# A gated causal convolution on one core: sixteen small GpSimd operations move to VectorE, and all queues get a new order

## The chip, the cores and the metric

The kernel runs on one core of a Trainium2 chip. The core has a matrix engine (TensorE, "PE" in the profile, with its weight loads as "PEld"), three elementwise engines (VectorE, "DVE"; ScalarE, "ACT"; GpSimd, "POOL") and a queue that only issues transfers (SyncE, "SP"). Each works through its own list of instructions in order, and they wait for one another through semaphores. The metric is the device time of one execution in microseconds (us); less is better.

## The reference

```python
def reference(x, w, w_o):              # x [2, 16000, 144], w [15, 144, 288], w_o [144, 144], bf16
    B, T, D = x.shape
    K = w.shape[0]; dil = 2; pad = (K - 1) * dil
    xp = jnp.pad(x, ((0, 0), (pad, 0), (0, 0)))
    h = jnp.einsum('btc,cd->btd', xp[:, pad:pad + T, :], w[0])
    for i in range(1, K):
        off = pad - i * dil
        h = h + jnp.einsum('btc,cd->btd', xp[:, off:off + T, :], w[i])
    f = h[..., :D]; g = h[..., D:]
    z = jnp.tanh(f) * _sigmoid(g)
    return z @ w_o
```

A causal convolution along time with 15 taps that lie two steps apart, from 144 channels to 288; tanh of one half times the sigmoid of the other; then a 144 by 144 projection.

## The kernel before

**Tiling.** The 32000 time steps are cut into 128 runs of 250, one for each partition, so a "tile" is one time step of all 128 runs. Of the 144 channels the first 128 fill the contraction of a matmul (tiles named XA); the 16 that are left over, called the odd ones here, are packed from eight time steps into one contraction of 128 (tiles named XB). Work goes by octets of eight steps; two octets make a pair, and each pair has two "units", one for the even and one for the odd steps in it.

**Fewer multiplications.** The convolution is computed with nested differences: sums of weights (WC, WS, WT, WD, WV) are formed once in the opening, differences of tiles (V, DU, DD, and across octets GX, GU, GV, GD) are formed by VectorE for each octet (L736, L806, L813, L818), and products that several outputs share are computed once on TensorE (all at L824) and spread: ScalarE copies a PSUM bank to another (L977), or evicts it to SBUF (L450 for two neighbouring banks in one instruction, L453 for two that do not lie side by side), and VectorE adds shared parts (L1004, L1078). GpSimd does the large adds UX (L1014, two to a unit, 60 in all).

**Gate and projection.** ScalarE evicts each finished pair of banks with sigmoid and tanh (TG), VectorE multiplies (Z, L851), a DMA transposes Z to ZT (L917), TensorE projects (L934), ScalarE evicts to OS (L877) and a DMA stores it (L945).

**How x comes in.** After an opening that loads x and the weights in five pieces each and transposes on TensorE (L592 to L606), x comes in chunks of 16 steps (Xr, L489). For each octet the 128 full channels are copied to a staging tile (STA) and transposed by DMA into XA (L691). For each chunk the 16 odd channels are packed into a tile C16: two of six columns are plain copies (`free_copy`, recorded at L877 as C<-Xr), and four are differences of steps two apart, which GpSimd computes at L668 (C<-Xr 128x256, 15 times). C16 is transposed by DMA (L670), written to a scratch tensor in DRAM (L678) and read back in the layout of XB (L703). In the opening a copy of 128x512 from XBh to XB stands on GpSimd (L634), in front of the first XB transfers.

**What sets the order.** The whole program is first written down as a graph of 2617 operations with their reads and writes. The order on each of the five queues is a list of operation numbers, worked out beforehand and kept in the source (`TABLE`, L20 to L94). `ON_ACT` (L95) names those `free_copy` operations that go to ScalarE instead of VectorE. When the program is built, `place` runs through the lists with assumed durations (`dur`, and for transfers `DMA_LAT`, `DMA_RATE` and `FIRST`); from this it takes which physical PSUM bank each product gets. Waits follow from the data alone: each operation waits for whatever wrote what it reads, and each queue is strictly in order, so an operation that waits holds up everything behind it on its engine. The flag `lock` marks operations which the planning keeps from overlapping between VectorE and GpSimd.

Of the kernel before, what the change touches and what calls it, by code (L numbers as in the profile page):

```python
# [5 lines left out]
ACT = mybir.ActivationFunctionType  # L6
ALU = mybir.AluOpType
# [5 lines left out]
DMA_LAT = 3.2  # L13
DMA_RATE = 280e3
FIRST = (1.12, 1.5)
# [78 lines left out]
}  # L94
ON_ACT = (110, 218, 275, 428, 430, 588, 908, 1067, 1227, 1393, 1702, 1704, 2023, 2182)  # L95


class _Op:
# [251 lines left out]
def _conv_wavenet_kernel(nc, x, w, w_o, out):  # L350
# [38 lines left out]
    with contextlib.ExitStack() as st:  # L389
# [74 lines left out]
        def bslot(o):  # L464
            return (o + 1) % NB
# [406 lines left out]
        def free_copy(dst, src, r, w, dur, alt):  # L872
            op = g.add("dve", lambda e: cast(op.eng, dst, src)(e), r=r, w=w, dur=dur, lock=True)
            op.alt = alt
# [514 lines left out]
```

## Time and profile before

| | |
|---|---|
| median of 3 runs | 308.64 us (308.09 to 308.67) |
| the profiled execution | 309.4 us |
| its span, first to last instruction | 307.6 us |
| granted TensorE clock | 1.00 of full speed |
| busy: TensorE, VectorE, ScalarE, GpSimd | 300.8, 279.9, 266.4, 111.4 us |
| matmuls | 2556 |

The profile records one execution. A row of the timeline reads: start, duration, engine, line of the kernel, operation, what is written from what, shape, count; in square brackets the time that the engine was idle before it and what ended the wait. `SPq` is the transfer queue at work. A busy time of TensorE overlaps from one matmul to the next, so its gaps are better seen in the starts.

### The profile page before, as it was taken

The numbers are of one execution on the slowest core, as the hardware profiler recorded it, in microseconds if no ns is written. First come the engines' busy times: TensorE is split into PE (matmuls) and PEld (weight loads), VectorE is DVE, ScalarE is ACT, GpSimd is POOL, SyncE is SP. The second block draws the span as 40 slices with busy tenths as digits, with TensorE's granted clock in tenths as the row PEclk, the third lists the DMA queues.
The fourth block names the chain that finished last, engine by engine and source line by source line (L and its number), as shares of the span: only waits on it lengthen the run. The fifth ranks groups of instructions, "written<-read, shape, count | busy, mean of one in ns | idle before, by whom it ended". The sixth has DMA issues, their size and how long they took to land.

```text
span 307.6 us, 7370 instructions
## 1 busy us (share of the span) xinstructions
PE 300.8 (98%) x2556; PEld 233.9 (76%) x2556; DVE 279.9 (91%) x604; ACT 266.4 (87%) x774; POOL 111.4 (36%) x105
## 2 busy tenths in 40 slices
PE   8899999999999999999999999999999999999995
PEld 7676677777677878877787788777777777877784
DVE  2999999999999999999998999999989799999755
ACT  2588799998879999998998999898898989988885
POOL 3494341333541244333224334313334332133330
PEclk9999999999999999999999999999999999999999
DMA  7959789989749999897767497977829997540543
GB/s 203 311 112 211 145 205 176 226 229 175 210 106 232 184 248 220 180 242 161 215 134 197 135 204 200 187 179 195 165 64 261 172 152 189 140 117 12 143 105 127
DMA packets 96719, 54.38 MB, mean 177 GB/s; under 512 B 83421, under 2 KB 86797, under 8 KB 96683
## 3 DMA queue, kind: packets, MB, share of 16 engines
q1 hardware_dynamic: 96137, 53.54, 77.2%
q0 software_dynamic: 512, 0.33, 0.5%
q8 instruction: 20, 0.33, 0.4%
q14 instruction: 16, 0.13, 0.1%
q10 hardware_dynamic: 34, 0.05, 0.1%
HBM read 15.93 MB, written 10.69 MB: 87 GB/s over the span
## 4 chain that ended last, share of the span: by engine, by line
PE 83%; DVE 10%; DMA 3%; SPq 1%; issue 1%; ACT 0%; DVEq 0%
PE PS L824 74%; PE PS L934 9%; DMA WA<-in_w_dram 2%; DMA XA<-STA 2%; DVE DD L736 1%; DVE V L736 1%; DVE DU L736 1%; DVE WC L646 1%; SPq L489 1%; DVE Xp L1004 1%; DVE Z L851 1%; DVE PS L1078 1%; DVE GU L806 1%; DVE WT L646 1%; DVE WD L646 0%
## 5 line engine op out<-in xcount | busy, mean ns | idle before, releaser
L1014 POOL TENSOR_TENSOR UX<-UC,XS 128x576 f32<-128x576 f32 x60 | 83.7, 1416 | 170.9 <-ACT UC L450 103.6
L824 PE MATMUL PS<-WB,XB 128*128 128x288 bf16 x360 | 102.2, 286 | 0.0
L824 PE MATMUL PS<-WA,GD 128*128 128x288 bf16 x450 | 88.3, 287 | 0.2
L977 ACT ACTIVATE PS<-PS 128x288 f32<-128x288 f32 x213 | 82.1, 415 | 4.4 <-PE PS L824 2.9
L450 ACT ACTIVATE TG<-PS 128x288 bf16<-128x288 f32 x204 | 73.0, 415 | 6.4 <-PE PS L824 5.3
L877 ACT ACTIVATE OS<-PS 128x432 bf16<-128x432 f32 (+1 forms) x93 | 42.7, 492 | 15.5 <-PE PS L934 14.9
L1004 DVE TENSOR_TENSOR Xp<-PS,UD 128x576 f32<-128x576 f32 x60 | 43.1, 751 | 10.7 <-PE PS L824 9.3
L1078 DVE TENSOR_TENSOR PS<-PS,Xp 128x288 f32<-128x288 f32 x120 | 50.8, 459 | 2.2 <-PE PS L824 0.6
L824 PEld LDWEIGHTS PS<-WA,GD 128*128 128x128 bf16 x450 | 41.0, 98 | 14.4 <-DVE PS L1078 1.6
L1078 DVE TENSOR_TENSOR PS<-PS,UX 128x288 f32<-128x288 f32 x120 | 50.0, 457 | 0.6
L824 PE MATMUL PS<-WS,GU 128*128 128x288 bf16 x210 | 44.6, 286 | 0.4 <-DVE GU L806 0.4
L934 PE MATMUL PS<-WOR,ZT 128*128 128x144 bf16 (+1 forms) x322 | 42.0, 254 | 0.0
L824 PEld LDWEIGHTS PS<-WB,XB 128*128 128x128 bf16 x360 | 35.2, 98 | 8.8
L824 PE MATMUL PS<-WC,GV 128*128 128x288 bf16 x210 | 37.8, 286 | 0.0
L824 PE MATMUL PS<-WD,DD 128*128 128x288 bf16 x210 | 34.7, 287 | 0.0
L934 PEld LDWEIGHTS PS<-WOR,ZT 128*128 128x128 bf16 x322 | 27.7, 98 | 6.2 <-issue 0.3
L851 DVE TENSOR_TENSOR Z<-TG 128x576 bf16<-128x576 bf16 (+1 forms) x63 | 28.1, 451 | 2.8 <-ACT TG L450 2.3
L736 DVE TENSOR_TENSOR V<-XA 128x1024 bf16<-128x1024 bf16 (+2 forms) x38 | 24.8, 655 | 0.1
L824 PE MATMUL PS<-WT,DU 128*128 128x288 bf16 x120 | 24.4, 287 | 0.4 <-DVE WT L646 0.4
L824 PEld LDWEIGHTS PS<-WD,DD 128*128 128x128 bf16 x210 | 19.6, 98 | 6.5 <-ACT PS L977 1.0
L824 PEld LDWEIGHTS PS<-WS,GU 128*128 128x128 bf16 x210 | 20.1, 98 | 5.9 <-DVE GU L806 0.7
L824 PE MATMUL PS<-WC,GX 128*128 128x288 bf16 x120 | 23.6, 286 | 0.0
(101 smaller groups left out, 437.5 us busy)
## 6 DMA issues: line engine op xcount, KB each, us to landing
Xr<-in_x_dram SPq DMA_DIRECT2D x15, 648.0 KB, 4.9
out_dram<-OS SPq DMA_DIRECT2D x30, 288.0 KB, 2.9
XB<-XB SPq DMA_DIRECT2D x29, 288.0 KB, 3.4
XB<-s SPq DMA_DIRECT2D x60, 48.0 KB, 3.0
s<-T SPq DMA_DIRECT2D x15, 96.0 KB, 3.0
WA<-in_w_dram SPq DMA_DIRECT2D x2, 288.0 KB, 5.5
ZT<-Z SPq DMA_TRANSPOSE x32, 3.4
Xp<-in_x_dram SPq DMA_DIRECT2D x2, 252.0 KB, 4.8
```

Source lines behind the costliest of these rows:

```text
L450: return e.activation(bass.AP(t[:].tensor, off + (0 if st > 0 else n), [[row, NP], [st, 2], [1, n]]), bass.AP(PS[:].tensor, lo * 512 + c0, ...
L489: return e.dma_start(tile_ap, src)
L646: g.add(eng, lambda v: v.tensor_tensor(dst(), a(), b(), ALU.add), r=r, w=wk, dur=dur, lock=True)
L736: return g.add("dve", lambda v: v.tensor_tensor(dst(), a(), b(), ALU.subtract), r=r, w=wk, dur=dur, prio=2, lock=True)
L824: return lambda t: t.matmul(bank(b), lhsT=lhs(), rhs=rhs(), start=start, stop=True, skip_group_check=True)
L851: g.add("dve", lambda v: v.tensor_tensor(dst(), TG[:, s, 1, 2 * k:2 * k + n, :], TG[:, s, 0, 2 * k:2 * k + n, :], ALU.mult), r=[("TG", s, ...
L877: return (lambda e: e.activation(dst(), src(), ACT.Copy)) if eng == "act" else (lambda e: e.tensor_copy(dst(), src()))
L934: return t.matmul(PS[:, c0:c0 + n * D], lhsT=ZT[:, zt, blk_, :], rhs=WOR[:, wi_:wi_ + n, :].rearrange("p a b -> p (a b)"), start=first, st ...
L977: g.add("act", lambda e: e.activation(bank(c), bank(b), ACT.Copy), r=[("bank", b)], w=[("bank", c)], dur=0.29, prio=prio)
L1004: return v.tensor_tensor(ue(u % NU, q, 0, 2).rearrange("p (v n) -> p v n", v=2), src, UD[:, u % NUD, :, :], ALU.add)
L1014: op = g.add("pool", lambda p: p.tensor_tensor(UX[:, u % NU, h, :, :], UC[:, 0, :, :], bass.AP(XS[:].tensor, h * N2, [[2 * N2, NP], [0, 2] ...
L1078: g.add("dve", lambda e, dst=dst, src=src, ua=ua: e.tensor_tensor(bank(dst), bank(src), ua(), ALU.add), r=[("bank", src), ("UX", us, h) if ...
```

## The change

Three things.

1. The subtraction of the odd channels (15 times) is recorded for VectorE, not GpSimd.
2. The 128x512 copy of the opening becomes a `free_copy`, an operation that stands on VectorE unless `ON_ACT` names its number. Its number is 82, and the new `ON_ACT` holds 82. `ON_ACT` as a whole goes from 14 to 18 numbers: of the octet copies to STA it names ten (four before), of the small copies to C16 seven (ten before).
3. All five lists are new, with the planning constants changed. GpSimd's list keeps the memsets, the 16 small weight transfers in another order, and the 60 large adds; its opening part has neither subtractions nor the copy. The functions `free_copy` and `cast` only move up in the source.

```diff
-DMA_LAT = 3.2
+DMA_LAT = 2.9
+SMALL = 1.45
 DMA_RATE = 280e3
-FIRST = (1.12, 1.5)
+FIRST = (1.12, 1.3)
...
-    "act": ("3 4 36 5 33 43 51 35 63 53 61 72 71 81 143 79 107 108 110 122 113 121 171 95 94 173 175 218 100 99 18 104 ...
+    "act": ("3 4 36 5 33 35 51 53 63 43 61 18 72 71 79 81 108 107 110 122 113 121 82 218 171 100 99 143 173 175 94 95 104 ...
...
-    "dve": ("1 0 30 31 34 146 41 42 155 138 130 131 156 144 132 52 157 133 139 149 134 140 163 135 136 62 150 147 148 141 137 158 160 ...
+    "dve": ("1 0 30 31 34 41 42 155 130 139 132 131 52 157 144 138 146 149 160 133 156 147 163 150 140 62 136 141 134 158 159 166 ...
...
-ON_ACT = (110, 218, 275, 428, 430, 588, 908, 1067, 1227, 1393, 1702, 1704, 2023, 2182)
+ON_ACT = (82, 110, 218, 430, 437, 590, 908, 915, 1065, 1225, 1227, 1234, 1393, 1543, 1545, 1702, 1711, 2021)
...
-            g.add("pool", lambda p: p.tensor_copy(XB[:, bslot(0), :, 0:2, :], XBh[:, 4:12, :].rearrange("p (a b) c -> p a b c", a=2)[:, :, 0:2, :]),
-                  r=[("XBh", 0)], w=[("XB", bslot(0), 0)], dur=0.7, lock=True)
+            free_copy(lambda: XB[:, bslot(0), :, 0:2, :], lambda: XBh[:, 4:12, :].rearrange("p (a b) c -> p a b c", a=2)[:, :, 0:2, :], [("XBh", 0)], [("XB", bslot(0), 0)], 0.2, 0.53)
...
-            g.add("pool", lambda p: p.tensor_tensor(cc[:, :, :, 2:6], xr(2), xr(0), ALU.subtract), r=[("Xr", s)], w=[("C16", s, 1)], dur=0.7, lock=True)
+            g.add("dve", lambda v: v.tensor_tensor(cc[:, :, :, 2:6], xr(2), xr(0), ALU.subtract), r=[("Xr", s)], w=[("C16", s, 1)], dur=0.56, lock=True)
...
-                  r=[("STA", q, 0), ("STA", q, 1)], w=[("XA", s)], dur=1.3, dma="xa", nbytes=8 * 128 * 128 * 2)
+                  r=[("STA", q, 0), ("STA", q, 1)], w=[("XA", s)], dur=1.3, dma="xa", nbytes=SMALL * 8 * 128 * 128 * 2)
```

`SMALL` multiplies the assumed size of the transfers that move 256-byte pieces (the three kinds of transposes and the write of S16); it stands only in the planning. In the lists above, 18 is the small activation that fetches the sigmoid table (L534), 33, 51, 61 and 71 are evictions of transposed XA tiles, 52 and 62 the memsets behind two of them (L606), 130 to 153 sums of weights (L646), and 155 to 169 the first tile differences (L736 to L818). In the parts left out, the subtractions stand in VectorE's list at places 36, 44 and 62 (the first three) and then 2 to 58 places apart; on SP the transposes, loads and stores change places with their neighbours, most by fewer than six.

More of the change, by code (lines that the diff above doesn't have):

```diff
@@ L608, in transposes, with free_copy, cast @@
             compact_pro(pi)
+        def free_copy(dst, src, r, w, dur, alt):
+            op = g.add("dve", lambda e: cast(op.eng, dst, src)(e), r=r, w=w, dur=dur, lock=True)
+            op.alt = alt
+        def cast(eng, dst, src):
+            return (lambda e: e.activation(dst(), src(), ACT.Copy)) if eng == "act" else (lambda e: e.tensor_copy(dst(), src()))
         hk = ["XBc_h%d" % i for i in range(5)]
@@ L667, in compact_chunk @@
             free_copy(lambda: cc[:, :, :, 0:2], lambda: xr(2, 2), [("Xr", s)], [("C16", s, 0)], 0.2, 0.31)
-            g.add("pool", lambda p: p.tensor_tensor(cc[:, :, :, 2:6], xr(2), xr(0), ALU.subtract), r=[("Xr", s)], w=[("C16", s, 1)], dur=0.7, lock=True)
+            g.add("dve", lambda v: v.tensor_tensor(cc[:, :, :, 2:6], xr(2), xr(0), ALU.subtract), r=[("Xr", s)], w=[("C16", s, 1)], dur=0.56, lock=True)
             if ci:
-                g.add("sp", lambda e: e.dma_start_transpose(T16[:, s, :, :], C16[:, s, :, :, :].rearrange("p a b c -> p (a b c)")), r=[("C16", s, 0), ("C16", s, 1)], w=[("T16", s)], dur=1.3, dma="xb", nbytes=3 * 32768)
+                g.add("sp", lambda e: e.dma_start_transpose(T16[:, s, :, :], C16[:, s, :, :, :].rearrange("p a b c -> p (a b c)")), r=[("C16", s, 0), ("C16", s, 1)], w=[("T16", s)], dur=1.3, dma="xb", nbytes=SMALL * 3 * 32768)
             else:
@@ L677, in compact_chunk @@
                       r=[("bank", tb)], w=[("T16", s)], dur=0.42)
-            g.add("sp", lambda e: e.dma_start(bass.AP(S16, ci * 384 * 128, [[128, NP], [128 * 128, 3], [1, 128]]), T16[:, s, :, :]), r=[("T16", s)], w=[("S16", ci)], dur=0.5, dma="xb", nbytes=3 * 32768)
+            g.add("sp", lambda e: e.dma_start(bass.AP(S16, ci * 384 * 128, [[128, NP], [128 * 128, 3], [1, 128]]), T16[:, s, :, :]), r=[("T16", s)], w=[("S16", ci)], dur=0.5, dma="xb", nbytes=SMALL * 3 * 32768)
         def load_xa(o):
@@ L870, in _conv_wavenet_kernel @@
         last_store = {}
-        def free_copy(dst, src, r, w, dur, alt):
-            op = g.add("dve", lambda e: cast(op.eng, dst, src)(e), r=r, w=w, dur=dur, lock=True)
-            op.alt = alt
-        def cast(eng, dst, src):
-            return (lambda e: e.activation(dst(), src(), ACT.Copy)) if eng == "act" else (lambda e: e.tensor_copy(dst(), src()))
         def ship_rows(h, dl):
@@ L917, in f @@
                 return e.dma_start_transpose(ZT[:, zt, d0:9, :], Z[:, z, d0 * 128:9 * 128])
-            g.add("sp", f, r=[("Z", o % NZ)] + [("Z", o % NZ, k) for k in keys] if keys else zkeys(o), w=[("ZT", zt)], dur=1.3, dma="zt", nbytes=(9 - d0) * 32768)
+            g.add("sp", f, r=[("Z", o % NZ)] + [("Z", o % NZ, k) for k in keys] if keys else zkeys(o), w=[("ZT", zt)], dur=1.3, dma="zt", nbytes=SMALL * (9 - d0) * 32768)
         GROUPS = ((0, 3), (3, 6), (6, 8))
```

146 rows, old and new, of the table TABLE are left out of this document.

## The prediction

> **What bounds the kernel now.** I read the page first, then busy time by stages, then TensorE's timeline wherever a stage was not full, and only then the engines that TensorE waited for.
>
> ```profile
> PE 300.8 (98%) x2556; PEld 233.9 (76%) x2556; DVE 279.9 (91%) x604; ACT 266.4 (87%) x774; POOL 111.4 (36%) x105
> ```
>
> ```profile
> 10.00:37.00 27.00, 25.16 (x215) 18.73 (x215) 26.85 (x57) 20.67 (x47) 15.59 (x26) 1.00 0.78 189
> 37.00:80.00 43.00, 43.00 (x358) 31.89 (x356) 41.19 (x90) 39.75 (x111) 15.03 (x12) 1.00 1.00 207
> 80.00:94.00 14.00, 13.45 (x112) 9.51 (x110) 13.90 (x30) 11.17 (x35) 7.04 (x6) 1.00 0.56 139
> 94.00:287.00 193.00, 193.00 (x1637) 152.54 (x1635) 181.37 (x386) 176.34 (x530) 65.46 (x51) 1.00 0.78 176
> 287.00:307.60 20.60, 17.50 (x165) 13.85 (x162) 13.40 (x33) 15.16 (x48) 5.29 (x4) 1.00 0.43 115
> ```
>
> The columns are stage, length, busy time of PE, PEld, DVE, ACT and POOL, then granted clock. TensorE is full from 37 to 80 and from 94 to 287 at clock 1.00. The change adds and removes no matmul, so in those 236 us a new order can lose time and cannot win any. Time can be won only where PE stops: in the opening, between 80 and 94, and near the end. In the two short stages that stop, DVE is nearly full (26.85 of 27.00, 13.90 of 14.00), so DVE is the one that holds TensorE back there.
>
> A matmul's busy time is a pipelined 286 ns; what counts is the step from start to start, and the chain of waits gives it: 7.23 / 59 = 0.1225 us.
>
> ```profile
> 71.97 5.28 DMA XA<-STA
> 77.27 0.43 DVE STA L877
> ...
> 279.55 7.23 PE PS L824 x59
> ...
> 288.88 0.62 DVE Xr L1295
> ```
>
> With that step, TensorE's timeline gives the length of each stop.
>
> ```profile
> 8.77 1.02 PE L824 MATMUL PS<-WA,XA 128*128 128x288 bf16 x7
> 10.52 0.30 PE L824 MATMUL PS<-WA,XA 128*128 128x288 bf16 x1 [0.73 <-DVE XA L606]
> ...
> 22.66 0.65 PE L824 MATMUL PS<-WA,XA 128*128 128x288 bf16 x4
> 24.07 0.30 PE L824 MATMUL PS<-WS,DU 128*128 128x288 bf16 x1 [0.77 <-ACT PS L977]
> ...
> 30.89 0.41 PE L824 MATMUL PS<-WT,DU 128*128 128x288 bf16 x2
> 31.69 0.30 PE L824 MATMUL PS<-WT,DU 128*128 128x288 bf16 x1 [0.39 <-DVE WT L646]
> ...
> 85.02 0.66 PE L824 MATMUL PS<-WV,V 128*128 128x288 bf16 x4
> 86.06 0.30 PE L824 MATMUL PS<-WS,GU 128*128 128x288 bf16 x1 [0.38 <-DVE GU L806]
> ...
> 289.32 0.53 PE L934 MATMUL PS<-WOR,ZT 128*128 128x144 bf16 x4
> 289.91 0.30 PE L824 MATMUL PS<-WA,GD 128*128 128x288 bf16 x1
> ```
>
> Seven matmuls from 8.77 end their steps at 9.63, the next starts at 10.52: 0.89 lost. Likewise 23.15 to 24.07 is 0.92, 31.14 to 31.69 is 0.55, 85.51 to 86.06 is 0.55, and near 289.7 about 0.2 (four half-width matmuls of at most 0.1 each from 289.32, the next start at 289.91; the memset of L1295 stands on the chain there). These are the 3.1 us that a better order can address; smaller stops I leave to the range.
>
> **The change part by part.** *The subtraction leaves GpSimd.* While GpSimd does it, some VectorE operations stretch:
>
> ```profile
> 16.55 0.98 POOL L668 TENSOR_TENSOR C<-Xr 128x256 bf16<-128x256 bf16 x1
> ...
> 18.57 0.62 POOL L634 COPY XB<-UX 128x512 bf16<-128x512 bf16 x1
> ...
> 19.65 1.09 POOL L668 TENSOR_TENSOR C<-Xr 128x256 bf16<-128x256 bf16 x1
> ...
> 27.76 1.25 POOL L668 TENSOR_TENSOR C<-Xr 128x256 bf16<-128x256 bf16 x1 [2.76 <-DMA Xr<-in_x_dram]
> ```
>
> ```profile
> 16.73 1.08 DVE L736 TENSOR_TENSOR DU<-XA 128x512 bf16<-128x512 bf16 x1
> ...
> 18.18 0.41 DVE L736 TENSOR_TENSOR DU<-XA 128x512 bf16<-128x512 bf16 x1
> 18.51 1.13 DVE L646 TENSOR_TENSOR WT<-WC 128x576 bf16<-128x576 bf16 x1
> 19.57 0.44 DVE L646 TENSOR_TENSOR WD<-WA 128x576 bf16<-128x576 bf16 x1
> ```
>
> The same 128x512 difference takes 0.41 alone and 1.08 beside a subtraction on POOL; a 128x576 sum takes 0.44 alone and 1.13 beside POOL's copy. Each meeting costs VectorE about 0.67. Counting the subtractions at 19.65 and 27.76 alike, the four meetings in the opening cost 2.7 us on an engine that has no idle time there. They vanish.
>
> *The subtraction arrives on VectorE.* No row shows it there. The nearest rows:
>
> ```profile
> L877 ACT ACTIVATE C<-Xr x10: 410/420/490, 18.4 to 242.5; 128x128 bf16<-128x128 bf16 x10
> L877 DVE COPY C<-Xr x5: 253/259/267, 60.3 to 195.5; 128x128 bf16<-128x128 bf16 x5
> L877 DVE COPY STA<-Xr x22: 413/421/427, 39.1 to 258.7; 128x1024 bf16<-128x1024 bf16 x22
> L877 ACT ACTIVATE STA<-Xr x4: 1042/1050/1070, 53.3 to 189.6; 128x1024 bf16<-128x1024 bf16 x4
> L668 POOL TENSOR_TENSOR C<-Xr x15: 858/876/1246, 16.6 to 235.9; 128x256 bf16<-128x256 bf16 x15
>   DMA Xr<-in_x_dram: 7.3, 5
> ```
>
> The strided copy of 128 elements from the same tile takes 0.26; successive VectorE operations overlap by some 0.08 (18.18 plus 0.41 ends 0.08 after the start at 18.51), so it occupies 0.18. Twice the elements occupy 0.36, if a second source is free: that is my value. [...] Fifteen times 0.36 is 5.4 us (2.7 to 10.8) over the run, three of them (1.1) in the opening.
>
> [...]
>
> *Copies trade places.* The new list of operations numbers the 128x512 copy among those that ScalarE takes, so it goes there, not to VectorE: about 0.6 by POOL's own row, in an opening in which ACT is busy 20.67 of 27.00. STA copies on ScalarE rise from 4 to 10, C copies fall from 10 to 7. ACT: 6 x 1.05 - 3 x 0.42 + 0.6 = +5.6 us on 266.4, with 41 idle. DVE: -6 x 0.34 + 3 x 0.18 + 5.4 less the stretches (2.7, and more later) is about +1, so the engine's total hardly moves. Cover: TensorE's own work, as long as VectorE stays ahead of it. Without cover a moved STA copy costs 1.05.
>
> *The new order, opening.* In the code's new list the activation that fetches the sigmoid table stands after the second of the large XA evictions; before, the load came in the middle of the gates:
>
> ```profile
> 21.89 1.28 ACT L450 ACT_TABLE_LOAD   x1
> ...
> 23.62 0.40 ACT L977 ACTIVATE PS<-PS 128x288 f32<-128x288 f32 x1
> ```
>
> The bank copy at 23.62 is what TensorE waits for at 24.07. With the load done near 13 the 0.92 goes. The load now delays the XA eviction behind it by about 1.3; its first reader in TensorE's new list comes some half a microsecond after that, so I cost it at nothing, and at up to 1.3 if that cover fails.
>
> Against this, VectorE's first adds are worse placed. The memset that TensorE awaits at 10.52 had two adds ahead of it after the weights landed and now has three:
>
> ```profile
> 9.56 0.46 DVE L646 TENSOR_TENSOR WD<-WA 128x576 bf16<-128x576 bf16 x1 [0.67 <-DMA WA<-in_w_dram]
> ...
> 10.39 0.07 DVE L606 MEMSET XA<- 128x16 bf16 x1
> ...
> 11.11 0.30 DVE L646 TENSOR_TENSOR WC<-WC 128x288 bf16<-128x288 bf16 x1
> ```
>
> Two such adds took 0.74 of the 0.83 up to the memset (0.46 less the overlap, each step 0.37); a 128x288 one (0.30, 0.22 without the overlap) comes on top, and I take +0.13, counting the rest of the 0.83 as slack that goes. Three more small ones (0.66), which filled the wait before 9.56, now follow it. That makes the next XA memset late by about 0.8; TensorE, later by 0.13 itself and with a stop of about 0.3 there already, loses perhaps 0.2 more. Together +0.35.
>
> VectorE from 9.6 to 34: -2.7 (meetings) +1.1 (subtractions) +0.8 (pushed adds) = -0.8. The sum behind the stop at 31.69 comes earlier by that, and in the new list five of the differences that stood ahead of it follow it, so I count the 0.55 as gone. What is late next is the second GD difference, behind them in the queue; it has a lead of microseconds now and I take it to keep most.
>
> *80 to 94.* VectorE fell behind because an STA copy waited for a transpose that took 5.28 us (77.27), and because one gate was stretched by POOL's subtraction. The new order puts the GU difference ahead of that unit's eight PSUM adds and the STA copy forty places later. The 0.55 goes. *The end.* The memset of L1295 (0.62 on the chain) stands far earlier in the list: -0.2.
>
> *Stops that the new order makes in the full stages.* From below 0 (nothing can be gained there), from above the 7.3 us below. I take 0.3: a transfer or two that lands late by a few tenths, as the smaller stops between 37 and 60 do now.
>
> **Sum** against the profiled execution, 309.4 (span 307.6 and 1.8 around it): -0.92 - 0.55 - 0.55 - 0.2 + 0.35 + 0.3 = -1.6, so 307.8 there. The median of the runs lies 0.76 below the profiled one: 307.0.
>
> **Rivals.** *The stops only move* (A). For it: TensorE is full for 236 us whatever the others do, and 1.6 us is the balance of a dozen small waits. Against it: three of the four have one visible cause each, and it is removed. Time 308.6.
>
> *VectorE waits for loads* (B, slower). GpSimd waited 7.3 us in five waits for Xr loads (the row above) and nobody minded. The same subtraction now stands in VectorE's queue, and behind it stand the PSUM adds that free TensorE's banks. It decides once a load lands later than its subtraction's turn by more than VectorE's lead. Against it: by the places of their neighbours nearly all subtractions stand 8 us or more behind their load's issue in the new lists. If half of the 7.3 reaches TensorE: 307.0 + 3.6 = 310.6.
>
> *VectorE and the large GpSimd adds collide* (C). Sixty remain:
>
> ```profile
> L1014 POOL TENSOR_TENSOR UX<-UC,XS x60: 1396/1408/1867, 35.5 to 297.4; 128x576 f32<-128x576 f32 x60
> ```
>
> Today VectorE does PSUM operations while these run and none is stretched much. A subtraction that starts during one would wait up to 1.4. Three such waits that reach TensorE: 307.0 + 4.2 = 311.2. [...]
>
> *STA copies on ScalarE hold up bank copies* (D). Six more at 1.05 each ahead of operations that TensorE awaits; half of them uncovered is 3.1: 310.1. Against it: four such copies run now between 53 and 190, where PE is full.
>
> **How the numbers follow.** What a measurement here can tell from no change is 0.2%, 0.6 us. My forecast has 0.56 (own range 305.6 to 308.0, all of it faster); A 0.22 (0.05 faster, 0.15 same, 0.02 slower); B 0.09, C 0.07 and D 0.06, nearly all slower. Faster 0.61, same 0.16, slower 0.23. The low end 305.6 is the whole 2.2 of stops without the costs, and 0.8 of the stop near 10 and the smaller ones, with the subtraction at its lower price; the high end 310.0 takes in A and most of D, and leaves out C and the worse half of B.
>
> **What would show it.** Right: no VectorE difference in the opening over 0.7 us; the table load before 16; no stop of TensorE near 23, 31 or 85; subtractions near 0.44 (0.36 and the overlap); stages from 37 on full. Wrong: subtractions on DVE with an idle time released by the Xr load (B), differences stretched beside L1014 (C), TensorE released late by the bank copies behind an STA activation (D), or the first real TensorE stop near 14 much over 0.5.

## The result and the profile after

The changed kernel takes 306.88 us in the median of six runs (306.55 to 307.07), the kernel before 309.15 us (308.09 to 309.87) beside it: a ratio of 0.9926, with an interval of 0.9904 to 0.9949. The profiled execution took 306.55 us with a span of 304.8. The first line below is from the page of the changed kernel, the others from its busy times by stages; the columns are as in the prediction.

```profile
PE 299.6 (98%) x2556; PEld 232.2 (76%) x2556; DVE 281.1 (92%) x616; ACT 269.8 (89%) x771; POOL 96.8 (32%) x89
```

```profile
10.00:37.00 27.00, 26.61 (x230) 20.19 (x228) 26.55 (x65) 22.07 (x51) 12.64 (x21) 1.00 0.78 191
37.00:80.00 43.00, 42.88 (x359) 32.40 (x358) 42.09 (x93) 38.81 (x112) 13.98 (x10) 1.00 0.86 201
80.00:94.00 14.00, 14.00 (x119) 10.63 (x117) 13.75 (x31) 12.63 (x40) 3.24 (x3) 1.00 0.84 196
```

Between 10 and 37 us TensorE now gets 230 matmuls started where it got 215, and between 80 and 94 us it is full, with 119 where it had 112. (In a second profile of the changed kernel, below, the first number is 222.) GpSimd is down by 14.6 us; VectorE is up by 1.2. The copy of 128x512 runs on ScalarE, so fifteen of the sixteen operations went to VectorE and one to ScalarE.

The timeline of the changed kernel shows what became of the places that the prediction named: TensorE near 14 and 23 us, then VectorE's first weight add, its first subtraction, and the memset of L1295.

```profile
13.82 1.15 PE L831 MATMUL PS<-WA,XA 128*128 128x288 bf16 x8 [0.26 <-DVE XA L607]
...
22.83 0.41 PE L831 MATMUL PS<-WB,UX 128*128 128x288 bf16 x2
23.08 0.53 PE L831 MATMUL PS<-WS,DU 128*128 128x288 bf16 x3
```

```profile
8.47 0.46 DVE L653 TENSOR_TENSOR WS<-WA 128x576 bf16<-128x576 bf16 x1 [0.87 <-DMA WA<-in_w_dram]
...
17.69 0.62 DVE L675 TENSOR_TENSOR C<-Xr 128x256 bf16<-128x256 bf16 x1
18.23 0.45 DVE L653 TENSOR_TENSOR WD<-WA 128x576 bf16<-128x576 bf16 x1
...
235.22 0.62 DVE L1295 MEMSET Xr<- 128x672 uint32 x1
```

The matmul on DU starts two steps of 0.1225 after the one at 22.83: the stop of 0.92 is gone. No VectorE operation is stretched any more. The subtraction holds VectorE for 0.54 us (17.69 to 18.23).

To compare whole kernels I use one more number, TensorE's **lost time**: the sum, over all successive matmuls, of the time between their starts less the step, taken as 0.1225 us for 288 columns and 0.062 to 0.064 for 128 or 144 (the medians of the steps are 0.122 to 0.123 for 288 columns, 0.062 for 144 and 0.056 for 128, in the profile before and in the one after). It is worked out from the records of all 2556 matmuls of a profiled execution, and its table by stage, in us, is what the experiments below are read with. Only differences between the rows count; the rows are single executions.

| profiled execution | 0 to 10 | 10 to 37 | 37 to 80 | 80 to 100 | from 100 | sum |
|---|---|---|---|---|---|---|
| before | 3.00 | 2.19 | 0.82 | 1.16 | 0.53 | 7.70 |
| changed | 2.28 | 1.02 | 0.82 | 0.08 | 0.65 | 4.84 |
| after_again (changed, a second time) | 2.80 | 1.76 | 0.98 | 0.08 | 0.65 | 6.28 |
| table_late | 2.76 | 1.27 | 0.99 | 0.08 | 0.65 | 5.74 |
| better | 2.67 | 1.01 | 0.98 | 0.08 | 0.76 | 5.52 |
| subs_back_fb | 3.01 | 2.13 | 1.24 | 0.08 | 1.20 | 7.66 |
| subs_only_fb | 2.27 | 2.57 | 1.18 | 1.27 | 2.04 | 9.34 |
| late_stages_fb | 2.08 | 1.84 | 1.36 | 0.80 | 0.29 | 6.37 |
| copy_back_early | 2.47 | 6.61 | 5.20 | 0.08 | 0.73 | 15.09 |

The stretch from 80 to 100 us repeats: 1.16 before, 0.08 in every profile of the new order. The opening doesn't: late_stages_fb has the opening of the kernel before unchanged and loses 3.92 us up to 37, where the kernel before lost 5.19; the two profiles of the changed kernel lose 3.30 and 4.56. So the traces locate about half of the gain of 2.3 us. The other half must lie ahead of 80 us, and these profiles don't show which stop it came from.

### The profile page after: what moved, and what is told of

The parts are those of the page before. It is cut to its first block, busy times and chain, and to the rows that moved or that the text cites. A ratio compares the mean times of both kernels' runs of the same rounds, so it can differ in the third digit from the quotient of the medians.

```text
span 304.8 us, 7337 instructions
## 1 busy us (share of the span) xinstructions
PE 299.6 (98%) x2556; PEld 232.2 (76%) x2556; DVE 281.1 (92%) x616; ACT 269.8 (89%) x771; POOL 96.8 (32%) x89
## 4 chain that ended last, share of the span: by engine, by line
PE 86%; DVE 5%; SPq 3%; ACT 2%; DMA 2%; issue 1%; ACTq 0%
PE PS L831 76%; PE PS L934 10%; SPq L710 2%; DMA WA<-in_w_dram 1%; SPq L490 1%; DMA XB<-s 1%; DVE V L743 1%; ACT TG L451 1%; DVE DD L743 1%; ACT PS L977 1%; DVE WC L653 1%; DVE WS L653 0%; DVE WD L653 0%; PE PS L894 0%; DVE C L675 0%
## 5 line engine op out<-in xcount | busy, mean ns | idle before, releaser
L977 ACT ACTIVATE PS<-PS 128x288 f32<-128x288 f32 x213 | 81.0, 416 | 3.9 <-PE PS L831 2.7
L451 ACT ACTIVATE TG<-PS 128x288 bf16<-128x288 f32 x202 | 71.7, 422 | 5.2 <-PE PS L831 4.3
L615 ACT ACTIVATE OS<-PS 128x432 bf16<-128x432 f32 (+1 forms) x93 | 43.5, 494 | 13.4 <-PE PS L934 12.8
L831 PEld LDWEIGHTS PS<-WA,GD 128*128 128x128 bf16 x450 | 39.9, 97 | 15.6 <-DVE PS L1078 1.6
L858 DVE TENSOR_TENSOR Z<-TG 128x576 bf16<-128x576 bf16 (+1 forms) x63 | 27.4, 441 | 2.5 <-ACT TG L451 2.3
L831 PEld LDWEIGHTS PS<-WC,GV 128*128 128x128 bf16 x210 | 19.0, 98 | 6.1 <-ACT PS L977 1.2
```

Of the source, the lines that this page charges most:

```text
L451: return e.activation(bass.AP(t[:].tensor, off + (0 if st > 0 else n), [[row, NP], [st, 2], [1, n]]), bass.AP(PS[:].tensor, lo * 512 + c0, ...
L615: return (lambda e: e.activation(dst(), src(), ACT.Copy)) if eng == "act" else (lambda e: e.tensor_copy(dst(), src()))
L831: return lambda t: t.matmul(bank(b), lhsT=lhs(), rhs=rhs(), start=start, stop=True, skip_group_check=True)
L858: g.add("dve", lambda v: v.tensor_tensor(dst(), TG[:, s, 1, 2 * k:2 * k + n, :], TG[:, s, 0, 2 * k:2 * k + n, :], ALU.mult), r=[("TG", s, ...
L977: g.add("act", lambda e: e.activation(bank(c), bank(b), ACT.Copy), r=[("bank", b)], w=[("bank", c)], dur=0.29, prio=prio)
```

## The experiments

Each was timed beside the kernel before, whose median was 309.12, 309.17, 308.75 and 309.21 us in the four sets.

### The changed kernel a second time

> The changed kernel itself, a second profiled execution, timed beside the kernel before. Theory: the 0.89 us stop of TensorE near 10 us, which is missing in the first profile of the changed kernel, depends on when the second weight transfer lands (VectorE was released by it at 9.56 us before and at 8.47 us after) and not on the order; then the first weight add on VectorE starts somewhere between 8.4 and 9.6 us here, and the sum of TensorE's lost time in the first 10 us lies between 2.3 us (first profile after) and 3.0 us (before). The ratio to before stays 0.990 to 0.995. Rival: the order itself removed the stop; then the transfer lands late again and TensorE does not stop near 10 us.

306.92 us, ratio 0.9915 (0.9894 to 0.9935). In this execution the weights released VectorE at 9.15, and TensorE stopped for 0.34 us near 10:

```profile
9.15 0.46 DVE L653 TENSOR_TENSOR WS<-WA 128x576 bf16<-128x576 bf16 x1 [1.37 <-DMA WA<-in_w_dram]
```

```profile
10.33 0.66 PE L831 MATMUL PS<-WA,XA 128*128 128x288 bf16 x4 [0.18 <-DVE XA L607]
...
33.59 0.42 PE L831 MATMUL PS<-WS,GU 128*128 128x288 bf16 x2 [0.74 <-DMA XB<-s]
```

So the stop near 10 follows the landing of the weights, which moves by a microsecond from one execution to the next (8.47, 9.15, 9.56), and its absence in the first profile was no gain of the order. The second row is a stop that the first profile has as 0.26 us: TensorE waits for the first XB transfers. What repeats in both profiles is 80 to 100 us: 0.08 lost in place of 1.16.

### The table load

In the changed kernel, the sigmoid goes back among the gates:

```diff
-"act": 3 4 36 5 33 35 51 53 63 43 61 18 72 71 ... 173 175 94 95 104 105
+"act": 3 4 36 5 33 35 51 53 63 43 61 72 71 ... 173 175 94 95 18 104 105
```

> The changed kernel, with only the sigmoid that triggers the table load put back to where the old list of ScalarE has it, in the middle of the first gates. Theory: the 1.28 us load again delays a gate activation, TensorE stops for 0.7 to 1.0 us between 21 and 25 us, and the time is 0.6 to 1.0 us over that of the changed kernel (ratio to before about 0.995 to 0.997). Rival (stops only move): other stops of the opening shrink by as much, and the time stays within 0.2 us of the changed kernel.

307.43 us, ratio 0.9942 (0.9924 to 0.9960), 0.5 us over the changed kernel in the same set; the intervals overlap, so this 0.5 is not shown. The stop itself is in the profile. From 23.43 plus two steps, 23.68, to 24.24 it is 0.57 us:

```profile
23.43 0.41 PE L831 MATMUL PS<-WB,UX 128*128 128x288 bf16 x2
24.24 0.54 PE L831 MATMUL PS<-WS,DU 128*128 128x288 bf16 x3 [0.41 <-ACT PS L977]
```

Then the converse, the kernel before with only this move:

```diff
-"act": 3 4 36 5 33 43 51 35 63 53 61 72 71 ... 218 100 99 18 104
+"act": 3 4 36 5 33 43 51 35 63 53 61 18 72 71 ... 218 100 99 104
```

> The kernel before with only the sigmoid that triggers the table load moved up in ScalarE's list, behind the third large XA eviction's predecessor as in the changed kernel, PSUM banks as before. Theory: the stop of 0.9 to 1.1 us near 22 to 23 us goes; what TensorE then meets is VectorE's lateness near 31 and 47 us, as in the run late_stages_fb, where 0.6 us came back there: 0.3 to 0.9 us under the kernel before, ratio 0.997 to 0.999. Rival (the stop only moves, all of it): ratio 0.999 to 1.001. Rival (the whole predicted 0.92 us stays): ratio 0.997 or less.

309.76 us, ratio 1.0030 (1.0010 to 1.0049): not faster at all. Its one profiled execution took 314.35 us, 4.6 over the median, so its rows can't explain the median, and why the gain didn't come is left open. One thing in them bears on the prediction: the wait for the bank copy near 24 is gone, and TensorE stops for 0.74 us at 15.57 instead, for an XA eviction that stands behind the table load on ScalarE. This is the delay that the prediction cost at nothing as long as its cover holds; in the changed kernel there is no such stop. What follows without the profile: the 0.92 us of this stop are not a term that can be had alone. In the new order the same move removes a stop of 0.57.

### Parts of the order

The opening of the changed kernel on the rest of the old lists (the first two lines say in words what was done to the lists):

```diff
-order of each engine: as in the changed kernel
+order of each engine: its operations that start before 37 us there, then all others in the old order
-g.add("dve", lambda v: v.tensor_tensor(cc[:, :, :, 2:6], xr(2), xr(0), ALU.subtract), ...
+g.add("dve" if ci < 3 else "pool", lambda v: v.tensor_tensor(cc[:, :, :, 2:6], xr(2), xr(0), ALU.subtract), ...
```

> The opening from the changed kernel (every operation that starts in the first 37 us there, with its engine and order), and everything after it in the order of the kernel before, with the subtractions after the third on GpSimd. Theory: the gain of the opening, 1.3 us of stops of TensorE between 10 and 40 us, stays, and the stops of 1.1 us between 80 and 100 us and of 0.2 us near 289 us are there as before: 1.2 to 1.6 us under the kernel before, ratio 0.995 to 0.996. Rival (stops only move): the rest of the list gives the time back, ratio 0.998 or more. Rival (all of the gain is in the opening): ratio 0.993, as the whole change.

311.24 us, ratio 1.0064 (1.0040 to 1.0087). And the changed kernel with the subtractions on GpSimd, in the lists too:

```diff
-            g.add("dve", lambda v: v.tensor_tensor(cc[:, :, :, 2:6], xr(2), xr(0), ALU.subtract), ... dur=0.56, lock=True)
+            g.add("pool", lambda p: p.tensor_tensor(cc[:, :, :, 2:6], xr(2), xr(0), ALU.subtract), ... dur=0.7, lock=True)
```

> The changed kernel, with the 15 subtractions back on GpSimd (each at the point of GpSimd's list that its start time in the changed kernel gives); all else as in the changed kernel. Theory: VectorE loses its own 15 x 0.54 = 8.1 us of subtractions, and gets back stretched operations where it meets GpSimd on them (4 to 6 us in all, up to 0.67 us each); the three meetings of the opening delay VectorE by up to 2 us where it is full and cost TensorE 0.2 to 0.6 us, and the rest is hidden: ratio to before 0.993 to 0.996. Rival (the move of engine is worth nothing by itself, the order is all): the time is within 0.2 us of the changed kernel. Rival (contention is the whole gain): the time goes back to the kernel before, ratio 0.998 or more.

310.53 us, ratio 1.0044 (1.0025 to 1.0063). The first lines of the two profiles show why neither result can be read as it stands (opening_only first, then subs_back):

```profile
PE 302.4 (98%) x2556; PEld 231.3 (75%) x2556; DVE 278.7 (90%) x607; ACT 270.5 (88%) x870; POOL 107.0 (35%) x101
```

```profile
PE 301.8 (97%) x2556; PEld 230.2 (74%) x2556; DVE 280.0 (90%) x601; ACT 271.7 (88%) x813; POOL 110.8 (36%) x104
```

ScalarE has 870 and 813 instructions, not 771. `place` gives out PSUM banks by its assumed times; with lists edited by hand it pairs fewer products in neighbouring banks, and each eviction of such a pair becomes two instructions. The edit had changed a second thing. In the runs whose names end in fb, and in copy_back_early, the banks are therefore written into the source as the unedited kernel has them:

```diff
+BANKS = {27: (...), ...}
-                if left[op] or len(pool) < len(op.opens):
+                if left[op] or not set(BANKS.get(op.idx, ())) <= set(q[1] for q in pool):
```

> The same edit as in the run subs_back (the changed kernel with its 15 subtractions on GpSimd), and now every PSUM bank is written down as the changed kernel has it, so that ScalarE has its 771 instructions again, not the 813 of that run. Theory: the move of engine counts by itself, most of all in the opening: VectorE operations are stretched again where they meet the subtractions, the transposes of the first compacted chunk wait longer, and TensorE loses 0.5 to 1.5 us more in the first 37 us, with little after 100 us: 307.5 to 308.6 us. Rival (the order is all, and what made the run subs_back slow was the split gates): 306.7 to 307.1 us. Rival (the banks did nothing): 310 us or more as in the run subs_back.

309.44 us, ratio 1.0010 (0.9995 to 1.0026). The banks were worth about one of the 3.6 us; the other 2.5 us, the whole gain, are lost by moving the subtraction back. That is well over my 307.5 to 308.6. The stretches are back: ten VectorE operations last 5.2 us longer in all than the lower quartile of their own forms. Eight of them stand beside L675 (3.9 us), and two stand where GpSimd only issues weight transfers (17.13 and 21.52, 1.4 us). And one row I had not thought of, the last of the next three (they are GpSimd's; TensorE's follow):

```profile
18.86 0.93 POOL L675 TENSOR_TENSOR C<-Xr 128x256 bf16<-128x256 bf16 x1
...
23.30 1.12 POOL L675 TENSOR_TENSOR C<-Xr 128x256 bf16<-128x256 bf16 x1
27.37 7.28 POOL L675 TENSOR_TENSOR C<-Xr 128x256 bf16<-128x256 bf16 x1 [2.95 <-DMA Xr<-in_x_dram]
```

```profile
19.84 0.34 PE L680 MATMUL PS<-ID,C 128*128 128x128 bf16 x3 [0.65 <-POOL C L675]
...
28.10 0.41 PE L831 MATMUL PS<-WV,V 128*128 128x288 bf16 x2 [0.34 <-DVE V L743]
```

The third subtraction took 7.28 us on GpSimd. TensorE waits for the first, which stands behind weight transfers on GpSimd, and for VectorE. Note also the table: 80 to 100 us stays at 0.08, so the gain of that stretch is the order's alone; it is lost again in others, most of all from 100 us on (1.20 in place of 0.53).

Now the move alone, in the kernel before (the lists change as the expectation says):

```diff
-            g.add("pool", lambda p: p.tensor_tensor(cc[:, :, :, 2:6], xr(2), xr(0), ALU.subtract), ... dur=0.7, lock=True)
+            g.add("dve", lambda v: v.tensor_tensor(cc[:, :, :, 2:6], xr(2), xr(0), ALU.subtract), ... dur=0.56, lock=True)
```

> The kernel before, with the 15 subtractions alone moved to VectorE (the first three where GpSimd started them, the others 0.8 us later), the copy left on GpSimd, all lists else and all PSUM banks as before. Theory: VectorE takes 15 x 0.54 = 8.1 us more and loses the stretches of about 4 us, so the move alone is worth about nothing: the stop of 0.9 us near 23 us stays, that near 85 us shrinks, 308.6 to 309.6 us (ratio 0.998 to 1.002). Rival (the move is the gain): 307 to 308 us. Rival (VectorE is full, and without a new plan its extra 4 us lands on TensorE): over 310 us.

312.51 us (310.33 to 314.81), ratio 1.0122 (1.0082 to 1.0163): the last of the three cases, VectorE is full and its extra work lands on TensorE. One such place, with the step of 0.1225 broken for 0.35 us in the middle of a stage that had been full:

```profile
146.21 0.90 DVE L1078 TENSOR_TENSOR PS<-PS,Xp 128x288 f32<-128x288 f32 x2
147.01 0.61 DVE L668 TENSOR_TENSOR C<-Xr 128x256 bf16<-128x256 bf16 x1
147.55 0.82 DVE L1078 TENSOR_TENSOR PS<-PS,UX 128x288 f32<-128x288 f32 x2
```

```profile
148.43 0.42 PE L824 MATMUL PS<-WA,GD 128*128 128x288 bf16 x2 [0.18 <-DVE PS L1078]
```

The subtraction stands between PSUM adds that TensorE waits for. Together the runs make a square, in us:

| | subtraction on GpSimd | on VectorE |
|---|---|---|
| old order | 309.2 | 312.5 |
| new order | 309.4 | 306.9 |

The move costs 3.3 with the old order and brings 2.5 with the new one; the order alone, over the whole kernel, brings nothing. "New order" here takes in the copy's move to ScalarE. (In the two mixed corners the subtractions stand where the other engine had started them. A list planned for that engine might do better; none was tried.)

Last, the two late stops by themselves, in the kernel before:

```diff
-"dve": ... 603 605 747 607 ... 691 765 729 609 749 ... 2057 2042 ... 2486 2550 2487
+"dve": ... 603 605 609 747 607 ... 691 765 729 749 ... 2057 2550 2042 ... 2486 2487
```

> The kernel before, with two operations of VectorE moved ahead in its list and nothing else: the GU difference that TensorE waits for near 85 us goes ahead of the STA copy that waits for its own transfer (from 85.3 to about 76.6 us), and the memset that stands on the chain near 289 us goes to about 237 us; PSUM banks as before. The opening is untouched, so this is also a second look at it. Theory: the stops of 0.54 us near 85 and 0.23 us near 289 us vanish and stay away: 0.6 to 0.9 us under the kernel before, ratio 0.997 to 0.998. Rival (stops only move): ratio 0.999 to 1.000, with a new stop behind each.

308.69 us against 309.17; the ratio of 0.9996 (0.9972 to 1.0021) leaves it open whether anything was won. The stops near 85 and 289 are gone from the profile, the one near 81 has grown, and two new ones stand at 47 and 48 us, where TensorE, 1.3 us earlier out of the opening, meets VectorE late:

```profile
48.77 0.42 PE L824 MATMUL PS<-WA,GD 128*128 128x288 bf16 x2 [0.21 <-DVE PS L1078]
```

### The copy of 128x512

The changed kernel with only this copy back on GpSimd:

```diff
-            free_copy(lambda: XB[:, bslot(0), :, 0:2, :], ...)
+            g.add("pool", lambda p: p.tensor_copy(XB[:, bslot(0), :, 0:2, :], ...)
-"act": ... 113 121 82 218 ...
-"pool": ... 208 201 199 203 205 ...
+"act": ... 113 121 218 ...
+"pool": ... 208 201 199 82 203 205 ...
```

> The changed kernel with only the copy of 128x512 into XB put back from ScalarE to GpSimd, at the point of GpSimd's list that its start time (19.65 us) gives, PSUM banks written down as the changed kernel has them. Theory: GpSimd issues weight transfers from 14.6 to about 22 us and reaches the copy later, VectorE's operations that meet it are stretched by 0.3 to 0.7 us once, and ScalarE is 0.52 us freer: 307.0 to 307.6 us, 0.1 to 0.6 over the changed kernel. Rival (this half of the change is worth nothing): 306.7 to 307.0 us.

316.46 us, ratio 1.0256 (1.0236 to 1.0276): 9.5 us over the changed kernel, where I had expected 0.1 to 0.6. The copy, 0.62 us in the kernel before, lasts 12.46:

```profile
20.40 12.46 POOL L642 COPY XB<-UX 128x512 bf16<-128x512 bf16 x1
```

To see whether its place was the cause, the same with the copy earlier (five places, not the eight that the expectation names):

```diff
-"pool": ... 207 213 210 208 201 199 82 203 ...
+"pool": ... 207 82 213 210 208 201 199 203 ...
```

> As the run copy_back_fb (the changed kernel with the copy of 128x512 into XB on GpSimd, PSUM banks as the changed kernel has them), with the copy eight places further up GpSimd's list, ahead of eight of its weight transfers, so that GpSimd reaches it near 17.0 us and not at 20.4. Theory from that run: GpSimd gets no step done while VectorE runs its operations without a gap, from about 9 to 32 us, so the copy again lasts until VectorE's first gap near 32 us, 10 us or more, and the time is over 313 us. Rival (who waits for whom is decided by the moment at which GpSimd arrives): the copy takes 0.6 us as at 18.57 us in the kernel before, one operation of VectorE is stretched by 0.4 to 0.7 us, and the time is 306.9 to 307.6 us. Rival (what cost 9 us there was the copy's place behind the transfers): the copy takes 0.6 us, and nothing is stretched.

316.81 us, ratio 1.0252 (1.0230 to 1.0275). Of this run, the copy on GpSimd; VectorE's last operation before its first gap and the one after; busy times by stages (VectorE is the third of the five); the transfer queue; and TensorE:

```profile
17.72 15.03 POOL L642 COPY XB<-UX 128x512 bf16<-128x512 bf16 x1
```

```profile
31.07 1.21 DVE L820 TENSOR_TENSOR GD<-DD 128x2048 bf16<-128x2048 bf16 x1
38.49 0.76 DVE L1004 TENSOR_TENSOR Xp<-PS,UD 128x576 f32<-128x576 f32 x1 [6.21 <-PE PS L831]
```

```profile
17.70:32.30 14.60, 13.90 (x114) 10.65 (x112) 14.58 (x32) 12.29 (x32) 14.60 (x2) 1.00 0.44 100
32.30:48.00 15.70, 9.46 (x50) 5.68 (x51) 6.47 (x15) 4.28 (x12) 7.26 (x11) 0.67 0.71 151
```

```profile
22.23 1.18 SPq L677 DMA_TRANSPOSE T<-C  x1
32.78 1.91 SPq L710 DMA_DIRECT2D XB<-XB  x3
34.73 1.97 SPq L710 DMA_DIRECT2D XB<-s  x4
```

```profile
37.55 0.66 PE L831 MATMUL PS<-WS,GU 128*128 128x288 bf16 x2 [5.93 <-DMA XB<-s]
38.01 0.44 PE L831 MATMUL PS<-WB,XB 128*128 128x288 bf16 x1
38.25 0.44 PE L831 MATMUL PS<-WS,GU 128*128 128x288 bf16 x1
```

VectorE runs 32 operations, all of bf16 with two inputs from SBUF, without a gap up to 32.28, none of them stretched, and GpSimd's copy ends half a microsecond after that. In copy_back_fb, where it starts at 20.40, it is the same: VectorE runs up to 32.38, the copy up to 32.86. Behind it the chain is plain. The XB transfer that reads the copy goes out at 32.78 (23.64 in the changed kernel); the transfers queued behind it on SP follow; TensorE stands still for 6 us. Then the granted clock is 0.67 up to 48 us, which is the other part of the loss: a step takes up to 0.24 us there (38.01 to 38.25).

### Making it better, and the price of the subtraction

The changed kernel with the sigmoid at the head of ScalarE's list, an XA memset and the first subtraction a little earlier:

```diff
-"act": 3 4 36 5 33 35 51 53 63 43 61 18 72 71
+"act": 3 4 18 36 5 33 35 51 53 63 43 61 72 71
-"dve": ... 156 147 163 150 140 62 136 ... 148 165 135 111 145
+"dve": ... 156 62 147 163 150 140 136 ... 148 111 165 135 145
-w=["SCR2"], dur=1.5, soft=(chain["act"],))
+w=["SCR2"], dur=1.5)
```

> The changed kernel with three moves in the opening: the sigmoid that triggers the second table load goes to the head of ScalarE's list, ahead of the first copy, so that one table load in the idle time before the first transfer serves both (two loads of 1.28 us become one); the memset of an XA tile goes two operations up VectorE's list, from 13.70 to about 12.1 us; the first subtraction goes two places up, from 17.69 to about 16.9 us. Theory: the stops of 0.2 us at 6.4, of 0.4 to 0.5 us at 13.4 and of 0.2 us at 18.1 go and come back only in part: 0.3 to 0.7 us under the changed kernel, 306.2 to 306.6 us. Rival (stops only move, and the weight transfers set the opening): 306.8 to 307.0 us, as the changed kernel. Rival (the copies need their own table back after the sigmoid): a table load follows, and nothing is won at 6.4 us.

307.08 us, ratio 0.9944 (0.9922 to 0.9966): the changed kernel's time. The stops near 14 and 18 are gone, and one of 0.40 us near 26, with VectorE late, is new: they moved. The table load did shrink to one (the rows are ScalarE's first), which TensorE had no use for:

```profile
1.78 1.28 ACT L535 ACT_TABLE_LOAD   x1 [1.78 <-PEq L1374]
3.08 0.23 ACT L535 ACTIVATE SCR<-SCR 128x32 bf16<-128x32 bf16 x1
4.56 0.31 ACT L559 ACTIVATE XS<-Xp 128x128 bf16<-128x128 bf16 x1 [1.25 <-DMA Xp<-in_x_dram]
```

The cost of the subtraction, by forms of its operands, chunk by chunk in turn:

```diff
-            g.add("dve", lambda v: v.tensor_tensor(cc[:, :, :, 2:6], xr(2), xr(0), ALU.subtract), ...
+            # chunk ci % 5: 0 as it is (L690); 1 sources contiguous (L689); 2 destination contiguous (L687);
+            #               3 both (L685); 4 as it is, channels innermost (L683)
```

> The changed kernel, with its 15 subtractions in five forms, three of each, all of 128x256 bf16: as it is; with both sources read as 256 neighbouring elements; with the destination written as 256 neighbouring elements; with both; and as it is but with the 16 channels as the innermost loop, so that the sources are read in runs of 16 neighbours. The forms two to four compute other values (they leave the gathering of the odd channels out). Theory: the scattered reads cost the time (elements 144 apart at the innermost loop): as it is 0.62 us, sources contiguous 0.29 to 0.35 us as the 128x256 V rows, destination contiguous 0.6, both 0.29, channels innermost 0.3 to 0.45. Rival: the destination in runs of four elements costs it: then the second form stays at 0.6 and the third falls to 0.3. Rival (any stride anywhere loses the fast mode): only both contiguous falls to 0.29. In every form the time of the kernel moves by less than 0.5 us.

```profile
L690 DVE TENSOR_TENSOR C<-Xr x3: 619/620/624, 17.9 to 166.3; 128x256 bf16<-128x256 bf16 x3
...
L689 DVE TENSOR_TENSOR C<-Xr x3: 281/284/288, 21.5 to 174.5; 128x256 bf16<-128x256 bf16 x3
L687 DVE TENSOR_TENSOR C<-Xr x3: 620/622/623, 29.3 to 190.3; 128x256 bf16<-128x256 bf16 x3
L685 DVE TENSOR_TENSOR C<-Xr x3: 278/285/285, 55.2 to 209.9; 128x256 bf16<-128x256 bf16 x3
L683 DVE TENSOR_TENSOR C<-Xr x3: 1324/1325/1325, 55.8 to 219.6; 128x256 bf16<-128x256 bf16 x3
```

The scattered sources cost the time, as the theory had it (0.620 us against 0.284 in the median); a destination in runs of four costs nothing (0.620 against 0.622). But with the channels innermost, where I expected 0.3 to 0.45, it is 1.32: there the destination steps by 48 bytes at every element, the one stride that only this form has (it was not tried by itself). The one run took 308.71 us, 1.8 over the changed kernel, so my bound of 0.5 us was missed as well. Its profile has TensorE stopped for 0.46 us at 142.46 and for 1.43 at 224.54, each 3 to 5 us after one of these longest forms began. Ahead of the second, a product Z that meets one of GpSimd's large adds takes 1.66 us at 221.73 in place of 0.45, which is what rival C describes; that it is the cause of the stop is inferred from the order in time.

## Why the prediction was right, and where its steps were not

The time, 307.0 predicted and 306.9 measured, is within what can be told, but half a microsecond of this agreement is luck: I took 1.6 off a median of 308.64, and over more runs the kernel before has 309.15, so the gain is 2.3. The steps:

- **Stop near 23 (-0.92).** Gone, and by the cause given: with the table load put back, a stop of 0.57 returns on TensorE. But as a term it was oversized, and in the old order the early load brings no time at all.
- **Stop near 31 (-0.55).** The WT sum is early (WT<-WS,WA at 23.94, before at 31.34). What is late next is not the second GD difference, as I wrote, but the first XB transfer (0.26 and 0.90 us lost in the two profiles), so the term was not won whole in the first and not at all in the second.
- **Stop near 85 (-0.55) and at the end (-0.2).** Gone in every kernel with the new order; between 80 and 100 us the order won 1.08, about twice the term, since the stops near 81 and 93 went too.
- **First adds worse placed (+0.35).** Near 14 the stop grew from 0.29 to 0.42 and 0.52, as sized. Near 10 I had +0.13 on a fixed 0.89; it is 0 and 0.34, and follows the landing of the weights.
- **New stops (+0.3).** From 100 us on 0.65 in place of 0.53, although the stop of 0.23 at the end is gone: some 0.35 is new there, about as sized.
- **The subtraction at 0.36.** Mis-sized: 0.54 each, so 8.1 us over the fifteen and not 5.4, inside 2.7 to 10.8. No run shows the prices behind the two ends of that range, the lower of which is also in the low end of 305.6; sub_forms shows 0.28 us with contiguous sources and 0.62 with scattered ones. I had doubled the strided copy and taken the second source as free; how much of the 0.62 is the second source no run separates.
- **ScalarE +5.6.** It was +3.4: the STA, C and XB copies came as priced, but the 213 bank copies show 81.0 us in place of 82.1 at the same mean, since overlaps count once, and the gates are 0.7 shorter.
- **A meeting costs VectorE 0.67.** Right as far as it goes: no stretched operation is left in the changed kernel, and 5.2 us of stretching return with subs_back_fb. The opening had one more than I counted, 1.01 in place of 0.30 at 15.19, where GpSimd only issued weight transfers; with it the opening lost 3.4 us and not 2.7. Who starts first doesn't tell who is held up: at 18.51 VectorE starts 0.06 us ahead of the copy and is the one that stretches (1.13 in place of 0.44); in copy_back_fb a VectorE operation starts 0.13 ahead of the copy (20.27 and 20.40), and it is the copy that lasts. The failing step is what I made of the meetings. I entered the moves at -2.7 + 1.1 + 0.8 and took nearly all of the gain from the order. The square shows that over the whole kernel neither brings anything without the other. And a meeting has another loser: in three runs it is GpSimd's operation that lasts, beside VectorE at work with next to no gap (7.28 us in subs_back_fb, 12.46 in copy_back_fb, 15.03 in copy_back_early).
- **Copies trade places.** Costed at 0.6 on ScalarE and nothing else. With everything else as in the changed kernel, GpSimd doing this copy costs 9.5 us, at both of the places tried; this dense opening of VectorE needs the copy elsewhere.

Of the signs that I had named for being right, two were not met: the subtractions take 0.62 us and not 0.44, and TensorE still stops shortly after 31 us, now for the XB transfer. So the sum was right partly by balance: the subtraction too cheap and the stop near 23 too dear on one side, the stages from 80 to 100 too small on the other, with the stop near 10 left to the landing of the weights. Of the rivals, A (stops only move) describes single moves well: better and late_stages_fb moved stops by 0.4 to 0.6 us and gained little or nothing that can be told. B showed itself only in subs_only_fb, where VectorE waited for an Xr load once, 1.8 us. C didn't happen in the changed kernel: no VectorE operation is stretched, and where a difference meets a large add (40.45), it is GpSimd's add that takes longer, 1.94 us in place of 1.40. D neither: the longest wait for a bank copy past 37 us, 0.28 at 50.95, has no STA copy ahead of it.

## What to carry to other kernels

A list of removed stops is not a sum: ask of each whether the engine that was late has room, and test terms in pairs, since a move that costs 3.3 us alone can bring 2.5 us with the order made for it. Here a GpSimd copy of 0.62 us lasted 12.46 and 15.03 us beside a stretch of VectorE without gaps, and with a transfer queue waiting for it the kernel lost 9.5 us: before work that a queue waits for goes to GpSimd beside such a stretch, time it there. When a planner's list is edited for an experiment, hold its other outputs (here the PSUM banks) fixed, and look at the instruction counts before believing the time.

## What the runs showed of the hardware that was not expected

- Beside back-to-back VectorE operations GpSimd's copy lasted 12.46 us (copy_back_fb) and 15.03 us (copy_back_early, over 32 of them in a row) and ended half a microsecond after the last of them, at 32.86 and 32.75; in the kernel before it took 0.62. There, with VectorE as dense (busy 3.96 of the 4.00 us from 18 to 22), it was VectorE that stretched (1.13 in place of 0.44 at 18.51) and GpSimd that got through. With the opening's lists unchanged, the first subtraction took 0.98 us on GpSimd in one execution (before) and 2.28 in another (late_stages_fb). What decides between the two outcomes no run here settles.
- VectorE operations were also stretched, by about 0.7 us each, where GpSimd only issued weight transfers (1.01 in place of 0.30 at 15.19 in the kernel before; 17.13 and 21.52 in subs_back_fb, 1.4 us in all). The changed kernel issues the same 16 transfers there and has no stretched operation, so the cause is open.
- The price of a bf16 subtraction of 128x256 on VectorE went with the strides of its operands (sub_forms): 0.28 us with contiguous sources, 0.62 with scattered ones, 1.32 in the form whose destination steps by 48 bytes.
